# Another order for the first pass of a fused attention and mixer kernel, and two bank-marking products left out

## The chip, the cores and the metric

One core of one Trainium2 chip runs the whole program in one launch. The metric is the device time of an execution in microseconds (us); less is better. The engines are TensorE (PE in the profile; its weight loads are PEld), VectorE (DVE), ScalarE (ACT), GpSimd (POOL) and SyncE (SP), which issues nearly all DMAs. Each works through its own queue in the order of the program and waits on semaphores for the others.

## The reference

An attention without softmax (eight heads, normalised by its root mean square) feeds a token-and-channel MLP mixer. All data are float32; B = 8 batches, S = 576 tokens, 8 heads of 64, model width 512.

```python
kv  = einsum('bhsd,bhse->bhde', k, v)
out = einsum('bhsd,bhde->bhse', q, kv)
rms = sqrt(mean(out * out, axis=-1, keepdims=True) + 1e-06)
x   = (out / rms * g_norm)            # (B,H,S,D) -> (B,S,H*D)

xt = x.transpose(0, 2, 1)
h  = maximum(xt @ w_tok1, 0.0) @ w_tok2         # d_tok = 256
u  = x + h.transpose(0, 2, 1)
h2 = maximum(u @ w_ch1, 0.0) @ w_ch2            # d_ch = 1536
result = u + h2
```

The four weight matrices arrive as float64 in the inputs of the program, and the kernel rounds them to float32 by itself.

## The kernel before, in words

The kernel has two passes. The **first pass** does the attention and the token mixing for pairs of batches (four pairs, 0 to 3); its results u go to DRAM. Beside it the weights of the channel MLP are rounded. The **second pass** is the channel MLP, in a scheme that replaces eight block products by seven and adds and subtracts blocks around them. It first does one group of tokens in a simple form (`channel1_once`, `channel2_once`), then eight groups in a two-level form (`channel1`, `channel2`, `outer`).

A recording layer keeps the order in which the Python code calls the engines. In the first pass that order is written out by hand, as lists of words which `play` (line 1059) works off: `start`, `middle`, `steady` (used twice) and `last`. Each stage overlaps the attention of one pair with the token mixing of the pair before it: middle is attention of pair 1 and mixing of pair 0, the first steady stage attention of pair 2 and mixing of pair 1, the second steady stage attention of pair 3 and mixing of pair 2. The words, with s a side (batch) of the pair, c a chunk of tokens (0 and 1 are the first batch, 2 and 3 the second, 4 the remainders of both), h or t one of two tiles of a chunk:

| word | what it issues | engine, line |
|---|---|---|
| kv s h | 20 products k by v for half the heads of one batch | PE L352 |
| e s h | copies that kv from PSUM into the tile kvp | ACT L124 |
| l s h, lq s | load k and v, or q (tile qT), for the next pair | SP L115 |
| a c | 32 products of q with kvp into two PSUM banks (tiles ps_o, for c = 4 ps_r; two buffers in all) | PE L389, L401 |
| g c h | "gain": multiplies a bank by g_norm into x | DVE L421 |
| q c h | squares a bank | ACT L425 |
| t c h | sums the squares per head | DVE L442 |
| m, r, i c | mean, root, and inverse (four operations) for a group of chunks: for (0, 1), or for (2, 3, 4) | DVE L447, ACT L452, DVE L456 to L461 |
| s c t | scales a tile of x by its inverse: 8 operations | ACT L475 |
| p c t | the same in one operation | POOL L479 |
| h s t, hr | token product 1 for a batch and half of d_tok (4 matmuls); hr adds the remainder and has ACT make the four relus | PE L509, ACT L121 |
| z i | seed: copies x into the PSUM bank of u i, so that the product adds to it | ACT L124 |
| u i | token product 2 (2 matmuls, 4 for i = 8); then x gets the bank, by a copy of ACT where i was seeded (2, 4, 6), else by an addition of DVE | PE L536, ACT L124 or DVE L118 |
| a number n | n steps of the rounding of the channel weights | below |
| "-" and a word | that step of the pair before | |

The banks of ps_h and ps_u come from one pool of four, those of kv from one of two. A square q and a gain g read the same bank one after the other: q c 0 and g c 1 come first, then q c 1 (which waits for g c 1) and g c 0 (which waits for q c 0); the next a starts when both banks are read.

The rounding (`decode`, line 149; `stream`, line 1048) takes a block of weights through seven operations: scale (ACT L163, reads the raw block that a DMA of SP brought), clamp (DVE L166), shift (L170), sign (L174), power (L183), lower (L187), both (L118). One step is one operation, but the step "lower" also issues the scale of the next block and the step "both" the DMA of the block four further on, into the buffer that "lower" frees. The first eight blocks have 768 elements per partition, the last six 1024.

In the second pass PSUM is split into a pool m of six banks (tag "m") and a pool c of two (`late["c"]`, line 1191). `channel2_once` uses four banks p1, p6, p7, p5: its products run in the order 1, 6, 2, 7, 5, 4, 3, where 7 and then 4 write p7, and 5 and then 3 write p5; DVE reads each bank after each product. In `outer`, the first product of a set writes bank a (from m); ACT copies (or DVE adds) that into a bank c (`read_first`, line 791), and product 2 later adds onto it in place, with `start=False`. Products of seven sets are laid out by places (`PLACE`, line 757); the first set alone fills the first places, with product 1 at place 0 and product 6, which adds into the same bank a, at place 3. Before those, two 128 by 384 products (lines 1221 to 1224), one ahead of place 0 and one in place 1, write the two banks c and are read by nobody.

Of the kernel before, what the change touches and what calls it, by code (L numbers as in the profile page):

```python
# [11 lines left out]
F32 = mybir.dt.float32  # L12
# [7 lines left out]
def kernel(  # L20
# [33 lines left out]
    P = 128  # L54
    B, S, DM = k.shape
# [11 lines left out]
    FQ = FH // 2  # L67
# [31 lines left out]
    w_ch1 = consts.tile([P, 4, 4, FQ], F32, name="w_ch1")  # L99
# [6 lines left out]
    def do(f, *a, **kw):  # L106
        return lambda: f(*a, **kw)

    late = {}
# [7 lines left out]
    def tensor_add(o, a, b, op=ALU.add, engine=nc.vector):  # L117
        keep(engine.tensor_tensor(out=o, in0=a, in1=b, op=op))  # L118
# [4 lines left out]
    def copy(o, a):  # L123
        keep(nc.scalar.copy(o, a))  # L124

    def matmul(*a, **kw):
        keep(nc.tensor.matmul(*a, **kw))  # L127
# [170 lines left out]
    def w2_of(n):  # L298
        i = {1: 0, 7: 1, 2: 2, 3: 3}
        return w_ch2[:, i[n]] if n in i else late["d2"][:, {5: 0, 6: 1, 4: 2}[n]]  # L300
# [318 lines left out]
    def m_psum(shape, name):  # L619
        return late["m"].tile(shape, F32, name=name, tag="m")  # L620
# [17 lines left out]
    def r_tile():  # L638
        return late["r"].tile([P, 2, DH], F32, name="r", tag="r")
# [63 lines left out]
    def channel2_once(g):  # L703

        shape = [P, 2, DH]
        x = xg[g]
        quarter = lambda i, j: x[:, 2 * i:2 * i + 2, ts(j, DH)]

        def product(n, ps, start, stop):
            for p in range(2):  # L710
                for s in range(NS):
                    matmul(ps[:, p], lhsT=late["once"][n - 1][:, s, p], rhs=w2_of(n)[:, s],
                           start=(start and p == 0 and s == 0), stop=stop,
                           skip_group_check=True)

        p1, p6, p7, p5 = (m_psum(shape, f"ps_w{n}") for n in (1, 6, 7, 5))
        t1, u2, u3 = (r_tile() for _ in range(3))

        def first():
            product(1, p1, True, False)  # L720
            copy(t1, p1)

        def sixth():
            product(6, p6, True, True)
            tensor_add(u2, p6, t1)

        def seventh():
            product(7, p7, True, False)
            tensor_add(u3, p7, u2)
            tensor_add(quarter(0, 1), quarter(0, 1), u2)  # L730
            tensor_add(quarter(1, 0), quarter(1, 0), u2)

        def fifth():
            product(5, p5, True, False)
            tensor_add(u3, p5, u3)
            tensor_add(quarter(1, 1), quarter(1, 1), u3)

        def second():
            product(2, p1, False, True)
            tensor_add(quarter(0, 0), p1, quarter(0, 0))  # L740

        def fourth():
            product(4, p7, False, True)
            tensor_add(quarter(1, 0), p7, quarter(1, 0))
            store(g, xg, 1)

        def third():
            product(3, p5, False, True)
            tensor_add(quarter(0, 1), p5, quarter(0, 1))
            store(g, xg, 0)  # L750

        return [first, sixth, second, seventh, fifth, fourth, third]
# [7 lines left out]
    def put(place, *steps):  # L760
        beside[place] += steps

    def outer(place, size, mul, to, base=None, act=copy, onto=False):

        banks, t = {}, {}

        def product(n, name, start, stop):
            if start:
                banks[name] = m_psum([P, size], f"ps_{name}")
            mul(n, banks[name], start, stop)

        def temp(n, bufs):
            t[n] = late["tmp"].tile([P, FQ], F32, name=n, tag=n, bufs=bufs)[:, :size]
            t[n] = fit(t[n])
            return t[n]

        def fit(flat):
            return flat if size == P else flat.rearrange("p (w t) -> p w t", w=W)

        def read(o, i, j):

            if base:
                tensor_add(o, fit(banks["a"]), base(i, j))
            else:
                copy(o, fit(banks["a"]))

        def read_first():
            banks["c"] = late["c"].tile([P, DM], F32, name="ps_c")[:, :size]
            read(fit(banks["c"]), 0, 0)

        def write(i, j, name, n):
            tensor_add(to(i, j), fit(banks[name]), to(i, j) if onto else t[n])

        def put_on(i, j, n):
            if onto:
                tensor_add(to(i, j), to(i, j), t[n])  # L800

        def take(i, j, name, act):
            if onto:
                tensor_add(to(i, j), banks[name], to(i, j))
            else:
                act(to(i, j), fit(banks[name]))

        def at(n, name, start, stop, *steps):
            def all_of():
                product(n, name, start, stop)  # L810
                for step in steps:
                    step()

            products[place + PLACE[n]] = all_of

        at(1, "a", True, False, read_first)
        at(6, "a", False, False, lambda: read(temp("u2", 2), 0, 1))
        at(5, "b", True, False)
        at(7, "a", False, False, lambda: read(temp("u3", 1), 1, 1))
        at(2, "c", False, True, lambda: take(0, 0, "c", act))  # L820
        put(place + PLACE[7] + (1 if onto else 2), do(put_on, 1, 1, "u3"), do(write, 1, 1, "b", "u3"))
        at(4, "a", False, True, lambda: take(1, 0, "a", copy) if onto else read(to(1, 0), 1, 0))
        put(place + PLACE[4], do(put_on, 0, 1, "u2"))
        at(3, "b", False, True)
        put(place + PLACE[3] + 1, do(write, 0, 1, "b", "u2"))
# [200 lines left out]
    def store(g, x, i):  # L1026
        x = x[g]
        if g < B:
            dma(out[g, ds(2 * i * P, 2 * P)].rearrange("(t p) e -> p t e", p=P),
                              x[:, 2 * i:2 * i + 2])  # L1030
        else:
            store_rest({B: x}, 2 * i)
            store_rest({B: x}, 2 * i + 1)
# [64 lines left out]
    for block in tok1[2:] + tok2:  # L1098
# [7 lines left out]
    start = [  # L1106
        "kv00 e00 l00 j14 w01 w11 w02 w03 w04 w05 w06 w07 w12 w13 w14 w15 w16 w17", "kv01 j10 e01 l01 f0",
        "a00 g00 q00", "a01 g01 q01 t00", "a10 g10 q10 t01 m0 r0", "a11 g11 q11 t10 i0 p00 p01",
        "kv10 j6 t11 m1 r1 e10 i1 s10 p11", "kv11 j2 e11", "h000 h001 h002 h003", "a20 g20 q20", "a21 g21 q21 t20",
        "h010 t21 m2 r2", "a30 g30 q30 i2 p20", "a31 g31 q31 t30", "h011 t31 m3 r3 p21", "a40 i3 p30 g40 q40 p31",  # L1110
        "h012 h013 t40 m4 r4 w21 i4 s40 lq0 l10 l11"]
    middle = [
        "kv00 e00 w31 w22 w23 w24", "h10 w25 w26 w27 f1 -lq1 l00 w32 w33 w34", "kv01 e01 l01 w41 w35 w36 w37",
        "h11 f2 w42 w43 w44", "hr w45 w46 w47 f3", "a0 q00 g01 q01 g00 t00 t01", "u0 z2 1", "u1 1",
        "a1 q10 g11 q11 g10 t10 t11 m0 r0", "u2 i0 1", "kv10 e10 z4 s00", "u3 1 s01", "kv11 e11 1",
        "u4 1 z6", "a2 q20 g21 q21 g20 s10", "u5 t20 t21 2", "a4 q40 g41 q41 g40 lq0 l10 l11", "u6 t40 t41 2",
        "a3 q30 g31 q31 g30 lq1 s11", "u7 t30 t31 m2 r2 1 i2 p20 p21 s30", "u8 1 s31"]

    def steady(n0, n1):
        return [  # L1120
            "kv00 l00 e00 1 -s40", "h00 3", "kv01 l01 e01 1", "h01 3", f"a0 q00 g01 q01 g00 {n0}",
            "h10 1 t00 t01 2", "h11 4", "hr 2 z2", "a1 q10 g11 q11 g10 1", "kv10 l10 e10 t10 t11 m0 r0 1",
            "u0 i0 1", "kv11 l11 e11", "u1 1 s00", "u2 z4 1", "a2 q20 g21 q21 g20", "u3 s01 t20 t21",
            "u4 z6 1", "a4 q40 g41 q41 g40 lq0", "u5 s10 t40 t41 1", "a3 q30 g31 q31 g30 lq1",
            "u6 s11 t30 t31 m2 r2 1 i2 p20 p21 s30", f"u7 1 s31 {n1}", "u8 2"]

    attentions = [attention(0, ((0,), (1,), (2,), (3,), (4,)))]
# [18 lines left out]
    for n in range(1, B // 2 - 1):  # L1146
        play(steady(*((3, 1), (0, 0))[n - 1]), attention=attentions[n + 1], mixing=mixings[n], before=attentions[n],
             rounding=rounding)
# [55 lines left out]
    n = len(sums1) // 3  # L1204
# [13 lines left out]
    fetch_x(1, 1)  # L1218


    for place in range(2):
        t = late["c"].tile([P, DM], F32, name="ps_c")
        step = do(matmul, t[:, :FQ], lhsT=w_ch1[:, 0, 0, :P], rhs=w_ch1[:, 0, 0], start=True, stop=True)
        put(place, step) if place else step()
    for n, (_, f) in enumerate(inner2):
        put(8 + n, f)
    for g in range(1, NG):
# [42 lines left out]
```

## Time and profile before

| | us |
|---|---|
| median of 6 runs (lowest, highest) | 807.76 (806.66, 807.91) |
| the profiled execution, its own time | 808.02 |
| its span, first to last instruction | 806.2 |
| TensorE matmuls busy | 787.5 |
| VectorE busy | 683.1 |
| ScalarE busy | 301.8 |
| GpSimd busy | 79.6 |

The stages of the first pass in that execution, by the start of their products on PE:

| stretch, us from the start of the span | what runs there |
|---|---|
| 0 to 40 | start |
| 40 to 79 | middle |
| 79 to 124 | first steady stage |
| 124 to 169 | second steady stage |
| 169 to 200.8 | last |
| 200.8 to 273.4 | `channel1_once` (ps_v), `channel2_once` (ps_w) |
| 273.4 to 806 | the marking products, then `channel1` and `channel2` for eight groups |

How to read it: in the timeline an entry gives start, length, engine, line, operation, out<-in, shapes, count, and in brackets how long the engine had been idle and what it waited for. Line numbers are often those of a helper (L127 is every matmul, L118 every addition on DVE, L124 every copy on ACT, L115 every DMA), so the names of the tiles tell which step it is: ps_kv for kv, ps_o and ps_r for a, ps_h for h, ps_u for u and z, x<-ps_o for g, sq<-ps_o for q, ms<-sq for t, w_ch or part for rounding, kvp<-ps_kv for e. A matmul in float32 counts as two in the profile (x2 is one). The chain that ended last is 83% PE, 8% DVE, 4% ACT and 3% DMA.

### The profile page before, as it was taken

To read this page: it belongs to the slowest core of one execution; us is meant where nothing else is said; L and a number is where in the kernel's file an instruction comes from. 1 tells how busy PE (TensorE), PEld (TensorE's weight loads), DVE (VectorE), ACT (ScalarE), POOL (GpSimd) and SP (SyncE) were. 2 spreads that over 40 slices of the span, in tenths; PEclk is the share of its full clock that TensorE was granted. 3 is DMA by queue.
4 is the path that set the end of the run, shared out by engine and by line. 5 is a ranking of instruction groups with operands and counts; after the bars stand their busy time and mean duration, and the time that the engine had idled before them with its cause. 6 is when DMAs were issued, how large, how long until landed. Compare 5 with 4: busy or idle time off the path is not lost.

```text
span 806.2 us, 17651 instructions
## 1 busy us (share of the span) xinstructions
PE 787.5 (98%) x7012; PEld 693.3 (86%) x7012; DVE 683.1 (85%) x1308; ACT 301.8 (37%) x838; POOL 79.6 (10%) x75
## 2 busy tenths in 40 slices
PE   6999999999999999999999999999999999999997
PEld 5645545544888899999999999999999999999997
DVE  4688989999786978978987997897898899799687
ACT  1357486674110134234234233332424323423331
POOL 1210101010000011012003003001100200300300
PEclk9999999999999999999999999999999999999999
DMA  9999997436448567368457648738836855763642
GB/s 292 330 345 334 340 358 297 150 122 206 157 170 297 188 213 244 125 221 263 157 203 234 205 148 261 237 118 248 276 120 214 262 169 184 248 200 123 218 147 83
DMA packets 97346, 175.51 MB, mean 218 GB/s; under 512 B 7024, under 2 KB 54128, under 8 KB 97264
## 3 DMA queue, kind: packets, MB, share of 16 engines
q1 hardware_dynamic: 95584, 172.65, 65.6%
q10 hardware_dynamic: 1680, 1.74, 0.7%
q8 instruction: 55, 0.90, 0.5%
q14 instruction: 27, 0.22, 0.1%
HBM read 137.79 MB, written 36.57 MB: 216 GB/s over the span
## 4 chain that ended last, share of the span: by engine, by line
PE 83%; DVE 8%; ACT 4%; DMA 3%; SPq 1%; issue 1%; ACTq 0%; DVEq 0%
PE ps_a L127 37%; PE ps_b L127 19%; PE ps_c L127 9%; PE ps_v L127 5%; PE ps_w L127 4%; PE ps_u L127 3%; PE ps_h L127 3%; ACT x L475 2%; DVE x L421 1%; DVE ms L442 1%; DMA raw<-in_moe_w_ch_dram 1%; PE ps_o L127 1%; DMA k_in<-in_k_dram 1%; DMA raw<-in_moe_w_tok_dram 1%; DVE part L187 1%; ACT sq L425 1%
## 5 line engine op out<-in xcount | busy, mean ns | idle before, releaser
L124 ACT COPY u<-ps_a 128x128 f32<-128x128 f32 (+1 forms) x160 | 56.0, 350 | 156.6 <-PE ps_a L127 156.6
L118 POOL TENSOR_TENSOR v<-v,v 128x384 f32<-128x384 f32 (+1 forms) x48 | 61.4, 1301 | 532.6 <-ACT v L124 492.8
L127 PE MATMUL ps_b<-uT,sums 128*128 128x128 f32 x672 | 86.2, 276 | 0.0
L127 PEld LDWEIGHTS ps_b<-uT,sums 128*128 128x128 f32 x672 | 80.7, 192 | 0.2
L118 DVE TENSOR_TENSOR v<-v,v 128x768 f32<-128x768 f32 (+1 forms) x86 | 79.4, 931 | 1.1
L127 PE MATMUL ps_a<-uT,w_ch 128*128 128x128 f32 x576 | 78.8, 275 | 0.0
L124 ACT COPY ps_c<-ps_a 128x128 f32<-128x128 f32 (+1 forms) x80 | 26.9, 336 | 129.6 <-PE ps_a L127 129.6
L118 DVE TENSOR_TENSOR v<-ps_b,u 128x384 f32<-128x384 f32 x112 | 61.4, 549 | 12.5 <-PE ps_b L127 10.7
L127 PEld LDWEIGHTS ps_a<-uT,w_ch 128*128 128x128 f32 x576 | 71.5, 192 | 0.4
L127 PE MATMUL ps_u<-h,w_tok 128*128 128x512 f32 (+1 forms) x160 | 68.0, 608 | 2.2 <-ACT h L121 1.2
L127 PE MATMUL ps_h<-x,w_tok 128*128 128x512 f32 (+1 forms) x160 | 66.0, 604 | 0.3 <-ACT x L475 0.3
L118 DVE TENSOR_TENSOR uT<-uT 128x512 f32<-128x512 f32 (+4 forms) x103 | 63.0, 628 | 0.8
L127 PE MATMUL ps_a<-uT,w 128*128 128x128 f32 x432 | 60.0, 275 | 0.0
L127 PEld LDWEIGHTS ps_a<-uT,w 128*128 128x128 f32 x432 | 54.0, 192 | 0.0
L127 PEld LDWEIGHTS ps_h<-x,w_tok 128*128 128x128 f32 (+1 forms) x160 | 25.9, 189 | 31.5 <-issue 28.3
L127 PEld LDWEIGHTS ps_u<-h,w_tok 128*128 128x128 f32 (+1 forms) x160 | 24.5, 179 | 32.5 <-issue 24.9
L121 ACT ACTIVATE v<-v 128x384 f32<-128x384 f32 (+1 forms) x86 | 42.5, 528 | 23.0 <-DVE v L118 22.5
L118 DVE TENSOR_TENSOR sv<-v 128x384 f32<-128x384 f32 x80 | 43.4, 550 | 9.0 <-ACT v L121 9.0
L118 DVE TENSOR_TENSOR xg<-xg,r 128x512 f32<-128x512 f32 x74 | 49.9, 684 | 0.7
L475 ACT ACTIVATE x<-x,inv 128x64 f32<-128x64 f32 x184 | 46.1, 338 | 9.6 <-DVE inv L461 9.6
L127 PE MATMUL ps_a<-sums,sv 128*128 128x128 f32 x336 | 47.0, 276 | 0.0
L127 PE MATMUL ps_a<-uT,sums 128*128 128x128 f32 x336 | 46.8, 275 | 0.0
(134 smaller groups left out, 1573.9 us busy)
## 6 DMA issues: line engine op xcount, KB each, us to landing
sums<-sums SPq DMA_DIRECT2D x112, 576.0 KB, 4.1
qT<-in_q_dram SPq DMA_DIRECT2D x8, 1152.0 KB, 9.7
xt<-u_dram SPq DMA_DIRECT2D x36, 256.0 KB, 3.9
blocks<-y SPq DMA_DIRECT2D x72, 128.0 KB, 2.7
uT<-blocks SPq DMA_DIRECT2D x36, 256.0 KB, 4.8
xg<-u_dram SPq DMA_DIRECT2D x18, 512.0 KB, 5.0
k_in<-in_k_dram SPq DMA_DIRECT2D x16, 512.0 KB, 9.1
u_dram<-x SPq DMA_DIRECT2D x16, 512.0 KB, 4.6
```

The costliest lines, as they stand in the source:

```text
L118: keep(engine.tensor_tensor(out=o, in0=a, in1=b, op=op))
L121: keep(nc.scalar.activation(o, a, AF.Relu))
L124: keep(nc.scalar.copy(o, a))
L127: keep(nc.tensor.matmul(*a, **kw))
L187: keep(nc.vector.scalar_tensor_tensor(out=part[0], in0=raw()[..., 0], scalar=2.0 ** -52, in1=part[0], op0=ALU.mult, op1=ALU.mult))
L421: keep(nc.vector.tensor_mul(x, bank[c, h], g_sb.to_broadcast([P, number(c), D])))
L425: keep(nc.scalar.activation(sq[c, h], bank[c, h], AF.Square))
L442: keep(nc.vector.tensor_reduce(stats_of(c)[0][:, h], sq[c, h], axis=AX.X, op=ALU.add))
L475: keep(nc.scalar.activation(x[:, k, h], x[:, k, h], AF.Copy, scale=inv[:, k, h]))
```

## The change

There are two parts.

In the second pass, p7 and p5 of `channel2_once` are taken from the pool c instead of m, so that their products are the first to write its two banks, and the two marking products are dropped. For this the tile in `read_first` gets the tag that the new ones have.

In the first pass the lists of middle and steady are written in another order; every word of them stays but one: in middle, s10 (ACT) becomes p10 (POOL). In steady, a1 with q, g, t, m and r of the first batch goes between the h products (h10, a1, h11, hr); kv10 and kv11 follow each other after hr; u0 and u1, u2 and u3, u4 and u5 are then pairs on PE, with a2, a4 and a3 between them. The seeds move as well: in steady z4 from ahead of a2 to behind s01, z6 from the words after u4 to behind s10; in middle z6 from behind u4 to ahead of it. The rounding steps move by a few places, their sum is unchanged: in middle one step less before a2 and two less before a4, which come later. With the step "both" moves its DMA: in middle one fetch of a raw block stands, on SP, behind the eight loads of l10 and l11 instead of ahead of them; in the first steady stage the later "both" keeps its place on SP, ahead of l10.

```diff
-        p1, p6, p7, p5 = (m_psum(shape, f"ps_w{n}") for n in (1, 6, 7, 5))
+        p1, p6 = (m_psum(shape, f"ps_w{n}") for n in (1, 6))
+        p7, p5 = (late["c"].tile(shape, F32, name="ps_c", tag="c") for _ in range(2))
...
-            banks["c"] = late["c"].tile([P, DM], F32, name="ps_c")[:, :size]
+            banks["c"] = late["c"].tile([P, DM], F32, name="ps_c", tag="c")[:, :size]
...
     middle = [
...
-        "a1 q10 g11 q11 g10 t10 t11 m0 r0", "u2 i0 1", "kv10 e10 z4 s00", "u3 1 s01", "kv11 e11 1",
-        "u4 1 z6", "a2 q20 g21 q21 g20 s10", "u5 t20 t21 2", "a4 q40 g41 q41 g40 lq0 l10 l11", "u6 t40 t41 2",
-        "a3 q30 g31 q31 g30 lq1 s11", "u7 t30 t31 m2 r2 1 i2 p20 p21 s30", "u8 1 s31"]
+        "a1 q10 g11 q11 g10 t10 t11 m0 r0", "u2 i0 1", "kv10 e10 z4 s00 p10", "u3 1 s01", "kv11 e11 z6 1",
+        "u4", "a2 q20 g21 q21 g20 s11", "u5 t20 t21 1", "a4 q40 g41 q41 g40 lq0 l10 l11", "u6 t40 t41 3",
+        "a3 q30 g31 q31 g30 lq1", "u7 t30 t31 m2 r2 2 i2 p20 p21 s30", "u8 1 s31"]

     def steady(n0, n1):
         return [
             "kv00 l00 e00 1 -s40", "h00 3", "kv01 l01 e01 1", "h01 3", f"a0 q00 g01 q01 g00 {n0}",
-            "h10 1 t00 t01 2", "h11 4", "hr 2 z2", "a1 q10 g11 q11 g10 1", "kv10 l10 e10 t10 t11 m0 r0 1",
-            "u0 i0 1", "kv11 l11 e11", "u1 1 s00", "u2 z4 1", "a2 q20 g21 q21 g20", "u3 s01 t20 t21",
-            "u4 z6 1", "a4 q40 g41 q41 g40 lq0", "u5 s10 t40 t41 1", "a3 q30 g31 q31 g30 lq1",
+            "h10 t00 t01 3", "a1 q10 g11 q11 g10", "h11 t10 t11 m0 r0 3", "hr i0 2",
+            "kv10 l10 e10 1", "kv11 l11 e11 z2", "u0 s00 1", "u1 2", "a2 q20 g21 q21 g20", "u2 s01 z4 t20 t21 1",
+            "u3 1", "a4 q40 g41 q41 g40 lq0", "u4 s10 t40 t41 z6 1", "u5 1", "a3 q30 g31 q31 g30 lq1",
             "u6 s11 t30 t31 m2 r2 1 i2 p20 p21 s30", f"u7 1 s31 {n1}", "u8 2"]
...
-    for place in range(2):
-        t = late["c"].tile([P, DM], F32, name="ps_c")
-        step = do(matmul, t[:, :FQ], lhsT=w_ch1[:, 0, 0, :P], rhs=w_ch1[:, 0, 0], start=True, stop=True)
-        put(place, step) if place else step()
```

## The prediction

> **What bounds the kernel now.** I read the page first, then busy times by stretch, then TensorE's (PE's) timeline in the first pass, then those of ScalarE (ACT) and VectorE (DVE) at each PE gap. The page and stretches:
>
> ```profile
> PE 787.5 (98%) x7012; PEld 693.3 (86%) x7012; DVE 683.1 (85%) x1308; ACT 301.8 (37%) x838; POOL 79.6 (10%) x75
> ...
> 79.00:124.00 45.00, 43.56 (x532) 22.52 (x530) 40.55 (x70) 29.22 (x90) 2.79 (x2) 1.00 1.07 354
> 124.00:169.10 45.10, 43.66 (x530) 22.35 (x526) 42.99 (x66) 29.88 (x87) 2.39 (x2) 1.00 0.55 200
> 169.10:200.75 31.65, 31.65 (x82) 13.17 (x80) 31.24 (x39) 17.13 (x43) 3.06 (x2) 1.00 0.50 160
> ```
>
> After the length the columns are PE, PEld, DVE, ACT, POOL busy, granted clock, DMA share, GB/s. PE sets the time; its chain has few holes. The changed stretches are the end of middle (60 to 79) and the two steady stages (79 to 124, 124 to 169); DVE is 90% and 95% busy in the latter, so it is the second bound. PE's timeline there, with the waits in brackets:
>
> ```profile
> 74.25 1.16 PE L127 MATMUL ps_o<-kvp,qT 64*64 64x64 f32 x64 [1.33 <-ACT sq L425]
> ...
> 102.58 1.98 PE L127 MATMUL ps_u<-h,w_tok 128*128 128x512 f32 x4 [1.17 <-ACT h L121]
> ...
> 112.73 1.98 PE L127 MATMUL ps_u<-h,w_tok 128*128 128x512 f32 x4 [0.21 <-ACT ps_u L124]
> ...
> 156.48 1.98 PE L127 MATMUL ps_u<-h,w_tok 128*128 128x512 f32 x4 [0.24 <-ACT ps_u L124]
> ...
> 162.52 1.16 PE L127 MATMUL ps_o<-kvp,qT 64*64 64x64 f32 x64 [1.12 <-ACT sq L425]
> ```
>
> These are a3 (middle), u0 and u4 (first steady), u4 and a3 (second): 4.07, with 0.13 ahead of the first steady a3 (117.18 to 117.31) 4.20. No more can be won here. Their causes:
>
> ```profile
> 73.81 0.38 ACT L425 ACTIVATE sq<-ps_r 128x256 f32<-128x256 f32 x1 [1.62 <-DVE x L421]
> ...
> 100.64 0.93 ACT L163 ACTIVATE w_ch<-raw 128x768 f32<-128x768 f32 x1 [8.33 <-DMA raw<-in_moe_w_ch_dram]
> 101.47 2.04 ACT L121 ACTIVATE h<-ps_h 128x512 f32<-128x512 f32 x4
> ...
> 112.09 0.58 ACT L124 COPY ps_u<-x 128x512 f32<-128x512 f32 x1
> ```
>
> a3 waits for a bank whose square waits for DVE; u0 for the relus, which stand behind a scale that waits for its raw block; u4 for its seed z4. The marking products:
>
> ```profile
> 273.38 0.81 PE L127 MATMUL ps_c<-w_ch 128*128 128x384 f32 x2
> 274.02 0.83 PE L127 MATMUL ps_a<-uT,w_ch 128*128 128x128 f32 x6
> 274.69 0.81 PE L127 MATMUL ps_c<-w_ch 128*128 128x384 f32 x2
> 274.89 0.46 ACT L124 COPY ps_c<-ps_a 128x384 f32<-128x384 f32 x1 [31.75 <-PE ps_a L127]
> 275.41 0.94 PE L127 MATMUL ps_a<-uT,sums 128*128 128x128 f32 x6
> ```
>
> **Marks.** They occupy 0.64 each. Without them product 1 starts at 273.38 and ends at 274.05. Product 6 adds into the bank that ACT is copying; the copy starts 0.20 after product 1's end, takes 0.46, product 6 follows 0.06 later: 274.77, not 275.41. So 0.64 is saved: the second mark hid that copy. Bounds: 0 (product 1 late too) and 1.36 (copy hidden elsewhere). p7 and p5 now lie in the c banks, so the copy also needs p7 read by DVE: 272.55+0.68=273.23, before the copy's 274.25; p5 is read by 276.42, its bank wanted at 277.9. Uncovered, a lateness of DVE would pass 1:1.
>
> **Middle.** Rounding steps cost, by start-to-start times of 84.81 to 91.95 and 71.97 to 73.30: clamp 0.59 (0.47 before a wait's end), shift 0.58, sign 1.00, power 0.59, lower 0.99, both 0.88. One "lower" moves from DVE's idle time ahead of a2 to behind t21; "both" and "clamp" move behind a4's gains. a4's gain starts 0.86+0.47-0.99=0.34 earlier, and a3 with it, 73.91: its wait shrinks to 0.99. But DVE runs unbroken from 70.18 to i2's end, now with 0.99 more. From there ACT runs unbroken (s30, scale, s31, e00, s40, e01, 81.24 to 88.18), so e01 ends at 89.17 and the first steady a0, which reads that kvp, starts at 89.23; PE is there at 88.86-0.34=88.52. New wait 0.71, net +0.37. Of s10's 2.0 on ACT nothing comes back, as ACT waits for DVE there; p10 costs POOL one multiply.
>
> While POOL ran two multiplies (81.29 to 84.08) DVE's lower and both took 1.49 and 1.70, not 0.96: 1.27 for two. p10 runs at 63 to 64.5; DVE idles 0.43 and 1.23 before a2's gain and has lost a 0.96 there, so 0.6 is covered; uncovered it would add to the 0.99. [...]
>
> SP: one raw fetch goes behind the eight loads l10, l11 (72.85 to 82.30). Issued near 82.3, landing after the slowest 9.56 (91.06 to 100.62), it is there at 91.9; ACT's scale takes its turn at 92.3, DVE's clamp at 97.5. Free. The loads go 1.0 earlier; qT, stores and later loads keep their order behind them.
>
> **First steady.** PE: a0 89.23, then a0 1.09, h10 3.63, a1 1.09, h11 and hr 5.35 (8.98 less 3.63), two kv 2.62: u0 at 103.01. DVE clamps until 90.99, then a0's gains 1.25, three steps 2.17, sums 1.19, three steps 2.44, a1's gains 1.25, sums 1.19, mean 0.10: 100.6. The root, ahead of the relus on ACT, ends at 101.05, the second relu at 102.07: u0 has 0.9 to spare, its 1.17 goes. The scale that waited for the raw block stands behind the relus; it delays e10, e11, z2, wanted at 106 by a2 and u2 (they end near 105.3). On SP the fetch after that block's both waits for DVE's lower, near 104.5 instead of 100.2, and l10, l11 and qT queue behind it, up to 4.3 later: the loads are wanted at 145, qT (117.03, then 121.3, landing after 9.7 at 131) at 133.7. Free, with 2.7 to spare.
>
> Then u0,u1 3.63 (106.64), a2 1.09 (107.73), u2,u3 3.63 (111.36, u2 out at 109.55), a4 0.63: u4's turn at 111.99. Its seed z4 now follows s01's eight scalings on ACT, and those q20, q21 and u2's copy. Before, DVE reached a2's gains at 112.45. Now: start +0.88, less lower 0.98 and both 0.88 (moved behind), less two idle stretches 0.41 and 1.78 (clamp at 101.60 waiting for that scale; gain at 104.54 waiting for a square behind the relus): 109.28. From the gain's end 109.97: q21 0.52, copy 0.46, s01 1.91, z4 0.58 (starts 112.61, 111.63 to 112.09, 113.72 to 115.63): 113.46. u4 starts at 113.52, a wait of 1.53 against 0.21. Behind it on PE stand u5, a3 and u6; for u4 itself wait, on ACT, its copy, s10 and the next seed z6. u4,u5 3.63, a3 1.09: 118.24; z6, behind u4's copy and s10, ends at 115.34+0.08+0.46+1.91+0.58=118.37; u6 at 118.43, before 118.59: -0.16. That contains some 0.7 from fewer switches (a single u takes 1.91, in a pair 1.815; a3 took 1.28).
>
> **Second steady.** ACT's u6 copy and s11 lead to i2, so DVE is 0.16 early too. a2's gains: 156.87-0.16-0.72-1.14 (power, lower moved behind)=154.85; no idle time to win. z4 ends at 155.55+3.47=159.02. PE reaches u3's end at 156.17-0.16-0.19=155.82; a4 waits for q21 to 156.23 and takes 0.86: 157.09; u4 at 159.08, a wait of 1.99. Then u4,u5 162.71, a3 without its 1.12, 163.80, z6 163.93, u6 163.99 against 163.61: **+0.38**. The last stage and all channel work are PE-bound without a gap to 275; they shift whole.
>
> **Sum.** +0.38-0.64=-0.26 us: span 806.2 to 805.9. That execution took 808.02, 1.82 around its span, and lies 0.26 above the runs' median 807.76; against the median I take **807.5**.
>
> The granted clock is 1.00 in every stretch, even where PE waited 6.3 for its first v_in, so the new waits are charged at their length. [...]
>
> **Rivals.** (a) DVE is earlier than my list, and the seeds wait only for ACT behind u2. Then z4 ends 3.03 after u2: u4 at 112.64 (-0.88), in the second stage at 154.0-0.88+3.09=156.21, not 159.08: -2.87, **804.6**. For: both floors are ACT's alone; a lower took 0.88 from start to start (93.54 to 94.42) where the next operation did not read it, not 0.99. Against: DVE had no idle time from 124 to 157. Half of it crosses the bound. (b) Slower: the two idle stretches, 2.19 together, come back in DVE's queue before a2's gains, with a1's gains and i0 still waiting for ACT. Every us then passes to u4, through u6, s11 and i2 to the second stage: 807.5+2.19=**809.7**; it decides from 1.9. For: each gain still waits for a square. Against: ACT is no longer held by the raw block then. (c) Slower too: that moved raw block lands so late that clamp, mean, root and relus wait; past 97.5 each us costs one, past the bound if it needs 17 us from issue: **809.6**; 9.9 is the longest median. (d) The move does nothing and only marks count: 807.1, inside the forecast's case.
>
> **Chances.** A measurement tells 0.2%, 1.6 us, from no change: 806.1 to 809.4. Forecast with (d) 0.46 (its own range 806.1 to 809.4), (a) 0.31, (b) 0.18, (c) 0.05: faster 0.31, same 0.46, slower 0.23. The range takes in (a) but for its last tenths, and (b): 804.9 to 809.7.
>
> **What would show it.** Right: product 6 about 1.4 after ps_w's end; u0 without wait; u4 waiting for ps_u by ACT 1.2 to 2 in both steady stages; a0 of the first waiting for kvp some 0.7; no a3 wait in the second. Wrong: u4 waiting 0.6 or less (then (a)), DVE idle before a2's gain, or an ACT scale waiting for raw ahead of the relus.

## The result, and the profile after

The changed kernel took 809.77 us (median of 15 executions, 808.22 to 811.09), the kernel before 807.35 (33 executions, 806.31 to 808.59): a ratio of 1.0029, interval 1.0023 to 1.0036. It is slower by 2.4 us (0.3%, clear of no change) where 0.26 less was forecast. The profiled execution took 810.5, its span is 808.7, 2.5 more than before.

The first line of the page's busy times, and the changed kernel's stretches (length, then PE, PEld, DVE, ACT, POOL busy, granted clock, DMA share, GB/s):

```profile
PE 788.5 (98%) x7008; PEld 693.9 (86%) x7008; DVE 682.6 (84%) x1308; ACT 300.2 (37%) x830; POOL 80.8 (10%) x76
```

```profile
89.00:123.50 34.50, 32.86 (x418) 16.79 (x420) 31.32 (x56) 22.07 (x61) 0.00 (x0) 1.00 1.03 345
123.50:154.00 30.50, 30.50 (x407) 16.85 (x404) 29.81 (x43) 18.03 (x51) 2.39 (x2) 1.00 0.65 239
154.00:172.20 18.20, 15.55 (x124) 6.41 (x122) 13.18 (x24) 11.87 (x36) 0.00 (x0) 0.81 0.36 125
172.20:203.90 31.70, 31.70 (x83) 13.20 (x81) 31.29 (x39) 17.11 (x43) 3.05 (x2) 1.00 0.50 160
```

Four matmul records fewer (two float32 products), and yet PE is busy 1.0 longer. The third row says why: at the end of the second steady stage the granted clock is 0.81, where the rows of the kernel before have 1.00. The loss lies there: the other rows have 1.00, and the last stage takes 31.70 as against 31.65. PE's timeline, with its waits in brackets:

```profile
73.86 1.16 PE L127 MATMUL ps_o<-kvp,qT 64*64 64x64 f32 x64 [1.10 <-ACT sq L425]
89.17 0.93 PE L127 MATMUL ps_o<-kvp,qT 64*64 64x64 f32 x48 [0.23 <-ACT kvp L124]
112.98 3.70 PE L127 MATMUL ps_u<-h,w_tok 128*128 128x512 f32 x8 [1.15 <-ACT ps_u L124]
118.09 5.57 PE L127 MATMUL ps_u<-h,w_tok 128*128 128x512 f32 x16 [0.32 <-ACT ps_u L124]
156.07 0.69 PE L127 MATMUL ps_r<-kvp,qT 64*64 64x64 f32 x32 [0.48 <-ACT sq L425]
158.94 6.77 PE L127 MATMUL ps_u<-h,w_tok 128*128 128x512 f32 x8 [2.17 <-ACT ps_u L124]
276.50 0.83 PE L127 MATMUL ps_a<-uT,w_ch 128*128 128x128 f32 x6
277.88 0.94 PE L127 MATMUL ps_a<-uT,sums 128*128 128x128 f32 x6 [0.55 <-ACT ps_c L124]
```

The waits stand where they were forecast: a3 of middle, a0, u4 and u6 of the first steady stage, a4 and u4 of the second. The two entries to compare are the third and the sixth: both are u4 and u5, the same eight records, and take 3.70 once and 6.77 once, 3.07 more. The same place by the clock:

```profile
156.00:158.00 2.00, 0.69 (x32) 0.56 (x32) 2.00 (x4) 2.00 (x9) 0.00 (x0) 1.00 0.06 16
158.00:160.00 2.00, 1.06 (x2) 0.55 (x3) 1.84 (x3) 2.00 (x5) 0.00 (x0) 0.58 0.34 131
160.00:162.00 2.00, 2.00 (x4) 0.96 (x3) 1.74 (x4) 0.50 (x2) 0.00 (x0) 0.50 0.35 131
162.00:164.00 2.00, 2.00 (x3) 0.67 (x2) 0.47 (x1) 1.19 (x4) 0.00 (x0) 0.50 0.00 0
164.00:166.00 2.00, 2.00 (x27) 0.70 (x29) 0.19 (x1) 1.79 (x7) 0.00 (x0) 0.72 0.00 0
166.00:168.00 2.00, 2.00 (x59) 1.33 (x51) 2.00 (x4) 0.80 (x2) 0.00 (x0) 1.00 0.30 105
```

A mean of 0.58 over 2 us is 1.68 at half clock, then 2, 2, and 1.12 (0.72): PE ran at half clock for 6.8 us, from 158.32 to 165.12. It began to do so in a stretch in which it had little to do: from u3's end (151.89+3.70=155.59) to u4 (158.94) are 3.35 us, and only a4's 0.69 lies in them. The page's row of the clock, in 40 slices of 20 us, shows nothing of this; it has a 9 in every slice. What u4 waits for, on ACT:

```profile
155.42 0.60 ACT L425 ACTIVATE sq<-ps_o 128x512 f32<-128x512 f32 x1 [2.81 <-DVE x L421]
155.92 0.58 ACT L124 COPY x<-ps_u 128x512 f32<-128x512 f32 x1
156.38 2.02 ACT L475 ACTIVATE x<-x,inv 128x64 f32<-128x64 f32 x8
158.30 0.58 ACT L124 COPY ps_u<-x 128x512 f32<-128x512 f32 x1
```

These are q21 (released by DVE's gain), u2's copy, s01 and the seed z4 (the rows are in order of start, and an entry may overlap the next by some tenths). That is the order that the lists now give: the seed is last.

The theory to test: the change itself is worth about what was forecast, and the rest is the clock, which falls because PE is nearly idle in one stretch of 3.35 us. Its rivals: the time is lost elsewhere in the new order, and the clock only shows it; or the clock falls for something else in the new order.

### The profile page after: what moved, and what is told of

The parts are those of the page before. It is cut to its first block, busy times and chain, and to the rows that moved or that the text cites. A ratio compares the mean times of both kernels' runs of the same rounds, so it can differ in the third digit from the quotient of the medians.

```text
span 808.7 us, 17639 instructions
## 1 busy us (share of the span) xinstructions
PE 788.5 (98%) x7008; PEld 693.9 (86%) x7008; DVE 682.6 (84%) x1308; ACT 300.2 (37%) x830; POOL 80.8 (10%) x76
## 4 chain that ended last, share of the span: by engine, by line
PE 85%; DVE 8%; DMA 3%; ACT 3%; issue 1%; SPq 0%; ACTq 0%; DVEq 0%
PE ps_a L127 37%; PE ps_b L127 19%; PE ps_c L127 12%; PE ps_u L127 5%; PE ps_v L127 5%; PE ps_h L127 3%; PE ps_w L127 2%; ACT x L475 2%; DVE ms L442 1%; PE ps_o L127 1%; DVE x L421 1%; DVE part L187 1%; DMA raw<-in_moe_w_tok_dram 1%; DMA u_dram<-x 1%; DMA k_in<-in_k_dram 1%
## 5 line engine op out<-in xcount | busy, mean ns | idle before, releaser
L127 PE MATMUL ps_u<-h,w_tok 128*128 128x512 f32 (+1 forms) x160 | 70.0, 627 | 4.2 <-ACT ps_u L124 3.6
L475 ACT ACTIVATE x<-x,inv 128x64 f32<-128x64 f32 x176 | 44.1, 339 | 7.3 <-DVE inv L461 7.3
```

Of the source, the lines that this page charges most:

```text
L475: keep(nc.scalar.activation(x[:, k, h], x[:, k, h], AF.Copy, scale=inv[:, k, h]))
```

## The experiments

Each kernel was timed beside the kernel before on the same chip; ratios are to that.

**One part of the change at a time.** First only the second pass's part:

```diff
 (the kernel before, with its lists of middle and steady)
...
+        p7, p5 = (late["c"].tile(shape, F32, name="ps_c", tag="c") for _ in range(2))
-    for place in range(2):
...
-        put(place, step) if place else step()
```

> Only the marking products are left out (p7 and p5 from the pool c); the first pass is in the order of before. Theory (the prediction's sum): product 6 follows product 1 after the copy into bank c, 0.64 us are saved, 806.7 against 807.35 (ratio 0.9992), and the trace shows one wait of product 6 of about 0.6 behind ACT's copy. Rival (the two banks of pool c cost something in channel2_once): no gain, or a loss, with a wait among the ps_c products before product 1.

Measured: 807.39 (11 executions, before 807.71), ratio 0.9997, interval 0.9988 to 1.0005. That holds the expected 0.9992 and also no change, so the times don't tell the marks' worth. The trace does: from ps_v's first product to product 1 are 72.62 us (198.91 to 271.53), as in the changed kernel (203.87 to 276.50, 72.63), against 73.27 before.

Then only the lists, with the marking products kept:

```diff
 (the kernel before, with the lists of the changed one)
```

> Only the new order of middle and steady; the marking products stay. Theory (half clock): the waits by themselves cost what was counted (+0.4), and in the second steady stage the 3.4 us between u3 and u4, with 0.69 us of products in it, are followed by some 6.5 us at half the granted clock, which costs about 3.1 more: 810.4 (ratio 1.004), a mean granted clock below 1. Rival (the order alone costs nothing, the loss comes with the c banks): 807.5 or less, ratio 1.000.

Measured: 809.74 (10 executions, before 807.71), ratio 1.0027, interval 1.0017 to 1.0036: the loss is in the lists. It is 0.7 below the 810.4 that was expected with some 6.5 us at half clock. Its u4, u5 and the clock behind them:

```profile
159.05 5.22 PE L127 MATMUL ps_u<-h,w_tok 128*128 128x512 f32 x8 [2.17 <-ACT ps_u L124]
```

```profile
156.00:158.00 2.00, 0.69 (x32) 0.56 (x32) 2.00 (x5) 2.00 (x9) 0.00 (x0) 1.00 0.09 29
158.00:160.00 2.00, 0.95 (x1) 0.50 (x2) 1.95 (x3) 2.00 (x6) 0.00 (x0) 0.68 0.28 106
160.00:162.00 2.00, 2.00 (x4) 0.90 (x3) 1.64 (x4) 0.60 (x3) 0.00 (x0) 0.50 0.41 156
162.00:164.00 2.00, 2.00 (x5) 0.68 (x4) 0.57 (x1) 1.35 (x5) 0.00 (x0) 0.96 0.00 0
```

The wait is the same 2.17, but the half clock lasted 1.28+2+0.16=3.44 us here, half as long, and cost 5.22-3.70=1.52, half as much. So in this place the clock's part is not one number; it differs between executions. The ten times say the same: four lie at 808.3 to 808.5, six at 809.6 to 810.7, and none between.

**The wait filled with work that nobody reads.** Eight 128 by 128 products go between a4 and u4 of the second steady stage:

```diff
+    def fill(n):
+        o = ps["kv"].tile([P, 2, P], F32, name="ps_f", tag="kv")
+        for _ in range(n):
+            matmul(o[:, 0], lhsT=w_tok1[:, 0, :P], rhs=w_tok1[:, 0, :P], start=True, stop=True)
...
-            "u3 1", "a4 q40 g41 q41 g40 lq0", "u4 s10 t40 t41 z6 1", "u5 1",
+            "u3 1", "a4 q40 g41 q41 g40 lq0", f"{f} u4 s10 t40 t41 z6 1", "u5 1",
```

> The changed kernel with 8 products of 128 by 128 that nobody reads (about 1.8 us) between a4 and u4 of the second steady stage, in a bank of kv; every wait stays. Theory (half clock after too little work on PE): u4 starts at the same time, about 158.9, but the clock stays at 1.00, u4 and u5 take 3.6 instead of 6.7: 809.8 less 3.1 is 806.7 (0.999), although PE does more. Rival (another reason than the clock): u4 and u5 stay slow, 809.8 or some more (1.003).

Measured: 808.00 (before 807.71), ratio 1.0005, interval 0.9996 to 1.0014. Its PE timeline from a4 on:

```profile
155.98 0.69 PE L127 MATMUL ps_r<-kvp,qT 64*64 64x64 f32 x32 [0.48 <-ACT sq L425]
156.60 2.05 PE L127 MATMUL ps_f<-w_tok 128*128 128x128 f32 x16
158.84 3.70 PE L127 MATMUL ps_u<-h,w_tok 128*128 128x512 f32 x8 [0.19 <-ACT ps_u L124]
```

u4 starts where it did (158.84), so nothing of the order's own wait is won. But u4 and u5 take 3.70, the clock is 1.00 from 152 to 166, and the loss is gone but for 0.3. Useless work makes this kernel 1.8 us faster (1.9 by the ratios, 1.0029 and 1.0005). That refutes the rival by which the time is lost elsewhere in the order. The median is 1.3 above what was expected, as that took the profiled execution's 3.07 for the usual one.

**Less filling.** Two products ahead of a4, in its own wait, so that u4's wait stays whole; and four behind a4, where the eight stood.

```diff
-            "u3 1", "a4 q40 g41 q41 g40 lq0", "u4 s10 t40 t41 z6 1",
+            "u3 1", f"{f} a4 q40 g41 q41 g40 lq0", "u4 s10 t40 t41 z6 1",
```

> The changed kernel with 2 unread products (128 by 128, about 0.45 us by the 8 that took 1.8) ahead of a4 in the second steady stage, so that they fall into a4's own wait of 0.48; the 2.17 wait of u4 behind a4 stays whole. Theory that the idle shares around a4 count together (0.69 us of products in the 3.42 us from u3's end to u4): the clock stays at 1.00, u4 and u5 take 3.70 instead of up to 6.77, u4 still starts at about 158.9 with a wait of about 2.2; time about 808.0, ratio to before 1.000 to 1.001, as with the 8 products behind a4. Rival, the 2.17 wait alone halves the clock: nothing changes, 809.8, ratio 1.003, and the clock in 160 to 164 is 0.50.

> The changed kernel with 4 unread products (0.9 us by the 8 that took 1.8) behind a4 in the second steady stage, where 8 took the wait away and 2 ahead of a4 left a median of 808.8. u4 still starts at about 158.5 to 158.9, with a wait of about 1.25. Theory that the stretch from u3's end to u4 counts as a whole: products now fill 1.6 of 3.4 us, against 1.1 with the 2 ahead and 0.69 without any; the clock falls in fewer executions than with the 2: median 808.0 to 808.4, highest below 809.5. Rival, that any idle time of more than 1 us can do it: as with the 2, a median of 808.8 and single runs to 810.7.

Measured with the two ahead: 808.79 (before 807.05), ratio 1.0019, interval 1.0011 to 1.0028, single executions from 807.25 to 810.67. With the four behind: 807.56 (before 807.50), ratio 1.0004, interval 0.9996 to 1.0013, from 807.30 to 808.45, less than the 808.0 to 808.4 expected of the median. First the two, then the four, in their traces:

```profile
155.00 0.61 PE L127 MATMUL ps_f<-w_tok 128*128 128x128 f32 x4
155.64 0.69 PE L127 MATMUL ps_r<-kvp,qT 64*64 64x64 f32 x32
158.50 3.70 PE L127 MATMUL ps_u<-h,w_tok 128*128 128x512 f32 x8 [2.17 <-ACT ps_u L124]
```

```profile
156.32 1.16 PE L127 MATMUL ps_f<-w_tok 128*128 128x128 f32 x8
158.56 3.70 PE L127 MATMUL ps_u<-h,w_tok 128*128 128x512 f32 x8 [1.08 <-ACT ps_u L124]
```

The profiled execution of the first kept its clock with a wait of 2.17 whole. Its median did not come down as expected, though. Only one execution of a kernel has a trace; for the others there are the time and the mean clock of the whole execution. A mean clock of 0.998 tells nothing, as the kernel before has 0.998 to 1.000; five of the twelve executions here have 0.996 or 0.997, so in part of them the clock still falls. Neither theory was right as put there. The clock falls more or less often, and in these kernels less often the more of the stretch is filled: above 809 us lie twelve of fifteen and six of ten executions with 0.69 us of products in it (the changed kernel, and the lists alone) and four of twelve with 1.17; with 1.79 none of eleven shows a fall by its time or mean clock.

**The same in the order of before.** One word is moved in the kernel before: z4 of the second steady stage goes behind q20 and q21, and in the other kernel behind s01 as well.

```diff
-            "u0 i0 1", "kv11 l11 e11", "u1 1 s00", "u2 z4 1", "a2 q20 g21 q21 g20", "u3 s01 t20 t21",
+            "u0 i0 1", "kv11 l11 e11", "u1 1 s00", "u2 1", "a2 q20 g21 q21 z4 g20", "u3 s01 t20 t21",
 (second steady stage alone; in the other kernel:)
+            "u0 i0 1", "kv11 l11 e11", "u1 1 s00", "u2 1", "a2 q20 g21 q21 g20", "u3 s01 z4 t20 t21",
```

> The kernel before with one word moved: z4 of the second steady stage stands behind q20 and q21 on ACT instead of ahead of a2. By the trace of before q21 ends near 158.5, so z4 ends near 159.05 and u4 starts near 159.1 instead of 156.48, after an idle time of 2.85 behind u3's whole 1.98 of products. Some 1.1 comes back at a3, whose wait is for DVE. Theory that any such stretch halves the clock (here 0.57 us of products in 3.42): the clock falls to 0.50 behind u4 for up to 6.5 us, and the time is 807.7+1.5+2 to 3 = 811.2 to 812.2, ratio 1.0045 to 1.0055. Rival, that the clock falls for something else in the new order: clock 1.00, 809.2, ratio 1.002.

> The kernel before with one word moved, further than last time: z4 of the second steady stage stands behind q20, q21 and s01 on ACT. With it behind q20 and q21 alone u4 started at 157.24 after a wait of 2.56, and single runs lay from 807.1 to 810.5. s01's eight scalings take 2.0 on ACT: u4 near 159.2 after a wait of 4.5, of which nothing comes back, as a3's wait is used up: 807.2+2.0=809.2 at full clock. [...] Rival, that the fall is a matter of chance in each execution that the length does not govern: lowest run 809.2, median about 810.

Measured with z4 behind q21: 808.69 (before 807.05), ratio 1.0017, interval 1.0008 to 1.0025, from 807.14 to 810.51. The wait is 2.56 and in the profiled execution the clock stays at 1.00. That misses both numbers: the wait itself cost next to nothing (the shortest five, 807.1 to 808.0 at clocks of 0.999 and 1.000, lie less than 1 above before), and the clock fell in only part of the executions (0.997 or 0.998 in the four above 809, where the highest of before, timed beside it, is 808.20). With z4 behind s01: 811.38 (before 807.50), ratio 1.0053, interval 1.0040 to 1.0067. The lowest is 811.10, where 809.2 was expected at full clock and as the rival's lowest, and the mean clocks are 0.995 to 0.997: the clock fell in each of the five executions after the wait of 4.46, against four of eleven after the one of 2.56, which speaks against the rival. u4 of the first and of the second kernel, and the clock around it in the second:

```profile
157.24 1.98 PE L127 MATMUL ps_u<-h,w_tok 128*128 128x512 f32 x4 [2.56 <-ACT ps_u L124]
159.70 3.47 PE L127 MATMUL ps_u<-h,w_tok 128*128 128x512 f32 x4 [4.46 <-ACT ps_u L124]
```

```profile
156.00:158.00 2.00, 0.00 (x0) 0.00 (x0) 2.00 (x4) 1.83 (x7) 0.00 (x0) 1.00 0.20 76
158.00:160.00 2.00, 0.30 (x1) 0.31 (x2) 2.00 (x3) 1.64 (x6) 0.00 (x0) 0.83 0.63 239
160.00:162.00 2.00, 2.00 (x3) 0.87 (x3) 0.13 (x1) 0.00 (x0) 0.00 (x0) 0.50 0.07 24
162.00:164.00 2.00, 2.00 (x35) 0.83 (x34) 0.11 (x1) 0.74 (x2) 0.00 (x0) 0.82 0.00 0
```

The half clock lasted 0.68+2+0.72=3.40 us and made 1.98 of products 3.47. So the fall needs nothing of the new order; a late seed in the old order has it too.

All kernels that differ in this stretch, side by side (the idle time is u4's wait, "filled" the products between u3's end and u4):

| kernel | u4's wait | filled, us | lowest, median, highest | lowest mean clock |
|---|---|---|---|---|
| changed | 2.17 | 0.69 | 808.22, 809.77, 811.09 | 0.994 |
| lists alone | 2.17 | 0.69 | 808.32, 809.74, 810.67 | 0.997 |
| 2 products ahead of a4 | 2.17 | 1.17 | 807.25, 808.79, 810.67 | 0.996 |
| 4 products behind a4 | 1.08 | 1.79 | 807.30, 807.56, 808.45 | 0.998 |
| 8 products behind a4 | 0.19 | 2.67 | 807.36, 808.00, 808.78 | 0.998 |
| before, z4 behind q21 | 2.56 | 0 | 807.14, 808.69, 810.51 | 0.997 |
| before, z4 behind s01 | 4.46 | 0 | 811.10, 811.38, 813.12 | 0.995 |

The idle time between u3's end and u4 sorts the table: with 2.65 in the first two kernels (0.48 and 2.17), 2.17 with 2 products and 2.56 with z4 behind q21 the clock fell in part of the executions, with 4.46 in all five, and with 1.56 (0.48 and 1.08) and 0.67 (0.48 and 0.19) no time or mean clock shows a fall. What decides between executions of one and the same kernel was not shown. At the ends of the traces, where PE has nothing to do, the time differs too: from the end of PE's last product to the start of half clock, worked out from rows of 1 us, it took 4.20 us in the kernel before (801.46 to 805.66; its row 805 to 806 has 0.83) and 2.89 in the changed one (803.95 to 806.84; its row 806 to 807 has 0.92). At the start of the program the rows have 1.00 while PE is idle for 6.3.

**The seeds ahead of the scalings.** If the late seed is the cause, the order can keep its gains without it:

```diff
-            ... "u2 s01 z4 t20 t21 1", ... "u4 s10 t40 t41 z6 1", ...
+            ... "u2 z4 s01 t20 t21 1", ... "u4 z6 s10 t40 t41 1", ...
```

> The changed kernel with z4 ahead of s01 and z6 ahead of s10 in both steady stages: one exchange on ACT's queue for each, nothing else. Theory (half clock through the seeds): each z4 ends 1.9 earlier, the waits of 1.15 and 0.32 in the first steady stage go, u4 of the second starts 1.5 plus 2.0 earlier, and without the long gap the clock stays at 1.00, which is worth another 3.1: about 803.3 (0.995), faster than both kernels. Rival (u4 and u5 are slow for another reason, such as late operands or banks): only the waits go, about 806.3 (0.9987), and u4 and u5 of the second stage still take 6.7 instead of 3.6.

Measured: 804.49 (before 807.71), ratio 0.9964, interval 0.9951 to 0.9976. That is 1.2 above the 803.3 expected, which again took 3.1 for the clock's usual part. Once more on another occasion:

> The version with the seeds ahead once more, beside the one with the middle's step moved, so that both stand against the same runs of before: 804.5, ratio 0.996.

804.19 (before 807.05), ratio 0.9958, interval 0.9946 to 0.9971. This is faster than both kernels. The waits that the seeds caused:

```profile
154.05 0.69 PE L127 MATMUL ps_r<-kvp,qT 64*64 64x64 f32 x32 [0.48 <-ACT sq L425]
155.02 3.70 PE L127 MATMUL ps_u<-h,w_tok 128*128 128x512 f32 x8 [0.28 <-ACT ps_u L124]
```

The 2.17 is 0.28, the 1.15 and 0.32 of the first steady stage are gone, and the clock is 1.00 from 152 to 160. Last, in the same version, one step of middle back into DVE's idle time ahead of a2:

```diff
-        "u4", "a2 q20 g21 q21 g20 s11", "u5 t20 t21 1", ...
+        "u4 1", "a2 q20 g21 q21 g20 s11", "u5 t20 t21", ...
```

> The version with the seeds ahead (804.49 before) with one rounding step of middle, lower, put back ahead of a2's gains, where DVE idles 2.22 us; the step count stays. If middle's end goes as the prediction's account of it: a3's wait in middle falls from 1.11 to 0.2 to 0.5, i2 ends about 0.95 earlier, the first steady a0 is not held (0.24 before), and everything behind it shifts by 0.8 to 1.0: time 803.6, ratio to before 0.995, 0.9 below the version run beside it. Rival: the shift is taken back at the next wait (u0, or a4 and u4 of the second stage, whose chain on DVE is without idle time): a3's wait falls, but u4 of the second stage waits 0.9 longer, and the time stays 804.5.

Measured: 803.76 (before 807.05), ratio 0.9957, interval 0.9945 to 0.9969. a3's wait is gone, the first steady a0 is still held for 0.25 (none was expected), u4 of the second stage still waits 0.28, and from the wait near 54 us, alike in both traces (54.70 and 54.50), to ps_v (196.28 and 196.95) it took 0.87 less. The medians of the two versions lie 0.43 apart with intervals that overlap, so the times don't settle it.

## Why the prediction was wrong

The failed step is the one on the clock: "The granted clock is 1.00 in every stretch, even where PE waited 6.3 for its first v_in, so the new waits are charged at their length." In the second steady stage the clock fell to 0.50. u6 was predicted for 163.99 and came at 166.73; ps_v came 3.12 later than before, not 0.38. "Every stretch" was read from rows too long to show it: the trace of before has half clock from 805.66 on, 4.20 behind PE's last product, and its row from 275.41 to 806.20 rounds that to 1.00. The 6.3 at the start was no evidence either: it is longer than the idle times at the ends of both traces after which the clock fell (4.20 and 2.89), so what the start shows does not hold behind busy work. The prediction also took the waits (0.41 and 1.99, together 2.4) one by one, when the clock fell in the stretch around both, 3.35 with 0.69 of work in it; its own times have that stretch (u3's end 155.82, u4 159.08).

The clock is not all of the miss. Between 0.26 less and 2.4 more lie 2.7 us; 1.9 of them go when the wait is filled. The rest fits a second term of the sum, u0's wait, which the point on the full clock below takes up.

The other steps, by the profiled execution:

- Marks: from product 1 to product 6 it takes 1.38, about the 1.39 that it took with a mark between (the copy is now waited for, 0.55), and the first mark's time is gone: 74.01 instead of 74.66 from ps_v to product 6, 0.65 less; 0.64 was predicted.
- Middle: a3 at 73.86 after 1.10 (predicted 73.91, 0.99). a0 was expected at 89.23 after a wait of 0.71; it started at 88.48 on the first half of the kvp, and waited 0.23 for the second, until 89.17. The time of e01 was right, but it held only three quarters of a0.
- First steady stage: u0 at 102.78 without wait (103.01), u4 at 112.98 after 1.15 (113.52, 1.53), u6 at 118.09 (118.43). Each a few tenths early.
- Second: a4 at 156.07 (156.23), u4 at 158.94 after 2.17 (159.08, 1.99), a3 without wait. Right.
- At full clock the forecast stands against the trace that it started from. From the wait near 54 us to ps_v it is 145.98 there (54.77 to 200.75), and 146.28, 146.26 and 146.27 in the kernels with 8, 2 and 4 unread products: 0.3 more, where 0.38 was forecast; u6 came at 163.95, 163.62 and 163.67 against 163.99. By their medians, though, the kernels with 8 and 4 took 0.3 and 0.1 more than before, against 0.26 less. The likely term is u0's wait of 1.17, counted as won: it hung on a raw block that landed at 100.6 in that execution. In three other traces with the order of before the scale that reads it starts at 98.76, 99.05 and 99.59, and u0 waits 0, 0 and 0.29; in the first of them, with the marks alone left out, the way to ps_v takes 144.48. How often u0 waits in the kernel before, no run shows.
- POOL beside DVE: the 0.6 for one multiply is half of the 1.27 by which DVE's lower and both were longer while POOL ran two. In that row POOL's multiplies took 1.06 (to 82.35) and 1.77 (to 84.07), DVE's lower ended at 83.16 and both at 84.89; the changed kernel has the same 1.49 and 1.70 (from 82.58 and 84.11) beside POOL's two multiplies (from 82.20). How the 1.27 came about, no run shows. Beside p10 nothing of it was seen: it ran from 63.26 to 64.50, and DVE's operations beside and behind it took 0.50, 0.69 and 0.95, as before.
- Rival (a), DVE earlier, did not come about: u4 waited as the forecast said. Rival (b) named 809.7, close to the time, but by another way: DVE's idle stretches did not come back, as the early u4 of the first stage shows. Rival (c): u0 did not wait for the moved block. None of the rivals named the clock.

On the size of the loss the runs agree: half-clock stretches of 3.44 and 3.40 us cost 1.52 (the lists alone) and 1.49 (z4 behind s01), and one of 6.8 cost 3.07. On its condition: 0.69 us of products in 3.35 did not keep the clock up, and in the order of before a wait of 2.56 was enough in part of the executions and one of 4.46 in all five. Why the profiled execution of the changed kernel had 6.8 us of half clock and that of the lists alone 3.44 stays open; the half clock began 0.62 ahead of u4 in the first and 0.33 in the second.

## What to carry to other kernels

Where PE has the chain, add up the waits on both sides of a small product, not each by itself: in this kernel a stretch of 3.35 us with 0.69 of products in it cost 3.07 us more than the waits in one trace and 1.52 in another (the lists alone), and nothing of the kind in some executions. One trace with a full clock does not show that a wait is safe: the traces with 2 products and with z4 behind q21 have 1.00 around waits of 2.17 and 2.56, while other executions of both have mean clocks down to 0.996 and 0.997. Read the clock by stretches of 2 us around each wait, as a page of 40 slices hides it. What releases a matmul (here a seed of 0.6 us) should stand on its engine ahead of work that is wanted later (here eight scalings of 2.0 us; the exchange took u4's wait from 2.17 to 0.28).

## What was not expected of the hardware

A gap of PE filled with eight unread products made the kernel faster, 809.77 to 808.00, as it kept the clock (1.00 from 152 to 166 in its trace, 0.50 in 160 to 164 without them). The fall of the clock differs between executions of one and the same kernel, which spans 808.22 to 811.09 with mean clocks from 1.000 to 0.994 (0.998 to 1.000 in the kernel before); behind PE's last product it comes after 2.89 us in the trace of the changed kernel and after 4.20 in that of before. And the arrival of one block moves between executions: the scale that waits for it starts at 100.64 in the trace of before (issued at 91.06, the block took 9.56) and at 98.76 in that with the marks alone left out, which makes a wait of 1.17 at u0 in the one and none in the other; a wait on a DMA that one trace shows is not safely there to be won.
